# Output weights laid out four times by TensorE instead of by 16 transfers, the first token tiles' turned x read in place, and the last batch's tail cut in another order

## The chip, the core and the metric

One core of a Trainium2 chip runs the whole program. It has TensorE (PE; its weight loads are listed apart as PEld), VectorE (DVE), ScalarE (ACT), GpSimd (POOL), SyncE (SP, which here only issues transfers) and 16 DMA engines. The metric is the device time of one execution in microseconds, as the median of several.

## What is computed

The reference first pools x with 32 inducing vectors by softmax attention, lets x attend to the pooled vectors, and sends the outcome through a layer with a softmax-gated hidden vector and a layer norm:

```python
h   = mab(I, x)                 # per batch: 32 x 128, from 12608 x 128
a   = mab(x, h)                 # 12608 x 128: softmax(x h^T / sqrt(128)) h
hid = a @ w_in                  # 1024 wide
solu = hid * softmax(hid)
ln  = (solu - mean) / sqrt(var + 1e-6) * g_ln
out = ln @ w_out                # 128 wide
```

There are 4 batches of 12608 tokens, all in float32 but the weights, which come as float64 and are rounded to float32 in the kernel.

## The kernel before

A **tile** is 128 tokens; a batch has 98 tiles and one half tile, 99 in all. The program is not written in the order in which it runs. A planner (class Planner) holds, for each engine, the operations that could start, with a cost in ns and a priority (smaller goes first), and emits them one by one; each engine then runs its own list strictly in that order and waits where an operand is late. So a constant changed in a cost or a priority moves instructions on all engines.

**Stage p1** (function p1) reads x in groups (12 tiles in batch 0, 16 later), turns it by TensorE (L629 in batch 0, by PE row groups at L597 later), copies it out of PSUM (L575, L608), stores the turned x to DRAM (L642), and keeps a running maximum, sum and pooled vector (scores L668, maximum L694, small steps L699 to L738, exponentials L758, transposition L778, gather L784, accumulation L816). Batch 0 has its whole p1 ahead of everything else; batch b+1's p1 groups are started by tile number while batch b runs, the first at tile P1_FROM, then every P1_STEP tiles. **combine** ends a batch's p1: it makes h (copied at L853) and h @ w_in (L867, copied to hs at L870).

**Stage p2** takes tiles in groups (4, 12, then 16): it loads the turned x back from DRAM (L899), makes scores (L919), transposes them on DVE (L926), reduces, subtracts on POOL (L931), exponentiates on ACT (L938), turns the weights by PE (L961) and copies them to aT (L976).

**Per tile** (functions main and soft), in this order: PE makes the hidden vector aT x hs (L1115, called mm1 below); DVE scales it and takes its extreme (L1157); ACT exponentiates (L1168); POOL multiplies (L1172); ACT sums the squares (L1183); DVE transposes into a group buffer vt (L1196). Four tiles are a **group** (the last of a batch has three); when all four are in vt, PE multiplies them with the output weights (L1244, called products below): 32 steps of 32x129 matmuls, with two of the four PE row groups for either half w. There are three vt buffers. mm1 uses two row groups and can run beside a products half.

**Finishing** (functions evacuate, finish, stored): products are copied from PSUM to SBUF (L1272, by DVE or ACT), and for FG = 5 groups together the layer norm's factor is worked out in some ten small steps on ACT and POOL (L1297 to L1311). It needs the tile statistics, which go through DRAM to change their layout (dd at L1213, dl at L1221). Then each group is scaled (L1318 on POOL, or L1322 on ACT) and stored (L1334; the three-tile group by six small stores, L1348).

**Weights** (functions rounded, weights_in, weights_out): float64 bits are turned to float32 by DVE (L424 to L433, L442), ACT (L435) and POOL (L438, L440, L445). w_out uses the same scratch buffers after w_in. Then ACT multiplies by g_ln (L467), PE takes the column means (L476), DVE subtracts them (L481), and 16 transfers (L497) lay the 128x1024 array out four times into wc, so that each PE row group has its copy. An Event wc_ready holds back the first products until then:

```python
for a in range(4):
    for q in range(4):
        c = yield dma(M * FF * 4, lambda: nc.sync.dma_start(rows[a*M:(a+1)*M, :, q, :C], wg[q*M:(q+1)*M]), d, o, issue=600, prio=LATE)
```

PSUM is used as eight early banks until batch 0's p1 is done; handover then frees them and makes four wide ones (Lock H), in which all later scores, mm1 outputs and products lie.

## Time and profile before

| | us |
|---|---|
| median of three timed runs | 1212.05 (1209.96 to 1212.18) |
| the profiled execution, its own time | 1207.19 |
| its span, first to last instruction | 1205.3 |

The profile shows one execution. A line such as L1244 is a line of the kernel before. "Idle before" names what ended an engine's wait. PE counts two records for each float32 matmul instruction. A granted clock of 1.00 is 2.4 GHz, 0.50 is 1.2 GHz. A PE that is busy is not PE at its peak, since two row groups count as much as four.

### The profile page before, as it was taken

What the parts mean: (1) busy time and instruction counts of PE and PEld (TensorE: products, weight loads), DVE (VectorE), ACT (ScalarE), POOL (GpSimd) and SP (SyncE); (2) the same over time, 40 slices, a digit from 0 to 9 for tenths busy, and PEclk for the clock granted to TensorE, in tenths of its full rate; (3) what the DMA queues carried; (4) which work ended last, traced back from release to release, by engine and by line L of the source; (5) the groups of instructions that cost most, each with busy time, mean ns of one, the idle gap of its engine ahead of it and who ended that gap; (6) DMA issues with size and microseconds to landing.
All of it is one profiled execution on the core that took longest, in us unless ns stands there. A gap on an engine that the chain in (4) does not pass through costs nothing. (4 is left out here: it accounts for less than half of the span.)

```text
span 1205.3 us, 78134 instructions
## 1 busy us (share of the span) xinstructions
PE 1159.9 (96%) x35487; PEld 1079.9 (90%) x35487; DVE 1098.2 (91%) x1701; ACT 1119.5 (93%) x2263; POOL 1050.5 (87%) x599
## 2 busy tenths in 40 slices
PE   9899999999999999999999999999999999999995
PEld 7679899998998999999889989989899999999995
DVE  5789989999998999999999999999999899999992
ACT  5598989999999999999999999999999999999994
POOL 2578879798999789899898889989899999999995
PEclk9959999999999999999999999999999999999998
DMA  9770433232324343323225243334121321212023
GB/s 352 256 211 11 131 90 110 83 107 61 83 63 130 100 115 110 109 67 93 54 69 153 76 140 111 84 100 119 40 70 18 83 66 20 75 21 49 5 49 87
DMA packets 171725, 113.63 MB, mean 94 GB/s; under 512 B 79072, under 2 KB 136320, under 8 KB 171264
## 3 DMA queue, kind: packets, MB, share of 16 engines
q1 hardware_dynamic: 171392, 108.63, 31.2%
q8 instruction: 277, 4.54, 1.6%
q14 instruction: 56, 0.46, 0.1%
HBM read 54.30 MB, written 52.18 MB: 88 GB/s over the span
## 5 line engine op out<-in xcount | busy, mean ns | idle before, releaser
L1244 PE MATMUL h<-wc,vt 32*128 32x129 f32 (+1 forms) x25600 | 996.2, 274 | 15.5 <-issue 6.2
L1244 PEld LDWEIGHTS h<-wc,vt 32*128 32x128 f32 (+1 forms) x25600 | 961.3, 185 | 46.9 <-issue 27.3
L1172 POOL TENSOR_TENSOR eu<-hn,eu 128x1024 f32<-128x1024 f32 x197 | 464.1, 2374 | 34.6 <-ACT eu L1168 33.9
L1115 PE MATMUL h<-hs,aT 32*128 32x128 f32 x6336 | 438.4, 278 | 7.2 <-DVE spare L1157 1.7
L1115 PEld LDWEIGHTS h<-hs,aT 32*128 32x128 f32 x6336 | 393.2, 190 | 26.2 <-issue 6.7
L1196 DVE STREAM_TRANSPOSE vt<-eu 128x1024 f32<-128x1024 f32 x330 | 402.2, 1230 | 7.6 <-POOL eu L1172 7.5
L1183 ACT ACTIVATE sq<-eu 128x1024 bf16<-128x1024 f32 x330 | 346.1, 1049 | 6.2 <-POOL eu L1172 1.9
L1172 POOL TENSOR_TENSOR eu<-spare,eu 128x1024 f32<-128x1024 f32 x133 | 314.1, 2373 | 35.3 <-ACT eu L1168 35.3
L1157 DVE TENSOR_SCALAR_CACHE_REDUCE spare<-h,rn 128x1024 f32<-128x1024 f32 x198 | 248.3, 1261 | 26.3 <-PE h L1115 12.4
L1157 DVE TENSOR_SCALAR_CACHE_REDUCE hn<-h,rn 128x1024 f32<-128x1024 f32 x198 | 248.1, 1261 | 15.9 <-PE h L1115 7.9
L1168 ACT ACTIVATE eu<-hn,nm 128x1024 f32<-128x1024 f32 x197 | 224.4, 1139 | 1.6 <-DVE hn L1157 1.0
L1172 POOL TENSOR_TENSOR spare<-spare 128x1024 f32<-128x1024 f32 x65 | 154.5, 2376 | 20.3 <-ACT spare L1168 19.4
L1168 ACT ACTIVATE eu<-spare,nm 128x1024 f32<-128x1024 f32 x133 | 151.5, 1139 | 0.6 <-DVE spare L1157 0.3
L1196 DVE STREAM_TRANSPOSE vt<-spare 128x1024 f32<-128x1024 f32 x66 | 81.0, 1228 | 0.0
L1168 ACT ACTIVATE spare<-spare,nm 128x1024 f32<-128x1024 f32 x65 | 74.0, 1138 | 0.3 <-DVE spare L1157 0.3
L1183 ACT ACTIVATE sq<-spare 128x1024 bf16<-128x1024 f32 x66 | 69.2, 1049 | 1.2 <-ACT sq L1183 0.4
L1318 POOL TENSOR_TENSOR spare<-spare,fin 128x512 f32<-128x512 f32 x61 | 61.8, 1040 | 1.5
L1183 ACT ACTIVATION_READ_ACCUMULATOR sq<-eu 128x1 f32 x330 | 62.6, 190 | 0.0
L597 PE MATMUL h<-ident,xn 32*128 32x32 f32 x1188 | 54.4, 227 | 0.5 <-issue 0.5
L597 PEld LDWEIGHTS h<-ident,xn 32*128 32x128 f32 x1188 | 51.1, 141 | 0.7 <-issue 0.4
L1272 ACT COPY spare<-h 128x774 f32<-128x774 f32 (+3 forms) x57 | 36.6, 644 | 13.2 <-PE h L1244 9.5
L1322 ACT ACTIVATE spare<-spare,fin 128x128 f32<-128x128 f32 x156 | 47.9, 390 | 0.8 <-POOL fin L1311 0.7
(165 smaller groups left out, 832.4 us busy)
## 6 DMA issues: line engine op xcount, KB each, us to landing
xT<-xd SPq DMA_DIRECT2D x96, 256.0 KB, 4.1
out_dram<-spare SPq DMA_DIRECT2D x96, 256.0 KB, 3.7
xn<-in_x_dram SPq DMA_DIRECT2D x73, 256.0 KB, 4.0
xd<-xT SPq DMA_DIRECT2D x72, 256.0 KB, 2.8
dl<-dd SPq DMA_DIRECT2D x396, 1.0 KB, 2.8
xd<-vt SPq DMA_DIRECT2D x7, 768.0 KB, 10.4
spare<-in_x_dram SPq DMA_DIRECT2D x5, 768.0 KB, 14.4
wc<-hn SPq DMA_DIRECT2D x16, 128.0 KB, 3.3
```

What stands on the lines that cost most here:

```text
L597: nc.tensor.transpose(out=tr[:, k * 512 + s * M : k * 512 + (s + 1) * M], in_=xn[r, s, :], identity=ident[r, r])
L1115: nc.tensor.matmul(hp[:, cols], lhsT=aT[rows, i // 2, :], rhs=hs[rows, cols], start=True, stop=True)
L1157: lambda: nc.vector.tensor_scalar(out=hn, in0=hp, scalar1=rn, scalar2=None, op0=ALU.mult, op1=ALU.min, accum_out=nm),
L1168: "ACT", 1133, lambda: nc.scalar.activation(e, hn, AF.Exp, bias=nm, scale=-1.0, accum_out=G["qe"][:, s, 1:2]), d, rel, srel,
L1172: d = yield Op("POOL", 2330, lambda: nc.gpsimd.tensor_tensor(out=e, in0=hn, in1=e, op=ALU.mult), de, prio=t + PR_MU)
L1183: "ACT", 1040, lambda: nc.scalar.activation(sq, e, AF.Square, scale=1.0 / 32.0, accum_out=G["qe"][:, s, 0:1]), d,
L1196: lambda: nc.vector.transpose(out=G["vtb"][:, : n * FF].rearrange("p (j s t) -> p j s t", j=M, s=n)[:, :, s, :], in_=e.rearrange("p (a f) ...
L1244: nc.tensor.matmul(op[:rows, a - 2 * w, :], lhsT=vt[q, k, :], rhs=wc[q, k, :], start=(k == 0), stop=(k == JB - 1))
L1272: return lambda: eng(to, at)
L1318: return lambda: eng.tensor_tensor(out=raw, in0=raw, in1=y[:, i0 : i0 + 4].unsqueeze(2).to_broadcast([rows, 4, C]), op=ALU.mult)
L1322: act(raw[:, a, :], raw[:, a, :], AF.Copy, scale=y[:, i0 + a : i0 + a + 1])
```

## The change

Seven things change; lines named from here to the end of this section are those of the changed kernel.

1. w_out has scratch buffers of its own (conv2, made of buffers that p2 and mm1 use later), so its rounding no longer waits for w_in's; its load and g_ln's go out among the first x loads. In rounded, the last step is one DVE instruction (L454) in place of a DVE compare and two POOL multiplications.
2. The four copies of w_out are made by eight matmuls with a 0/1 matrix (L544) into early PSUM banks and eight copies from PSUM (L522), four on ACT and four on DVE as planned. The ones column of wc is set once the first two p1 groups are done, and handover waits for wc_ready.
3. p2 of batch 0 has groups of 4 and 8, and reads these 12 tiles' turned x from the SBUF buffer of the first p1 group. The first group's scores and its turn (whole array, L1026) use early banks. Stores of batch 0's turned x wait until all of batch 0's x is loaded.
4. In the last batch the three-tile group comes before the last full one, and the last finish has that one group alone, the one before it four.
5. Full-group stores of batches 0 to 2 take one of the four transfer tokens (BULK) that x loads, turned-x stores and turned-x loads share.
6. The planner's costs of p1 and p2 steps and its priorities are other numbers; mm1 may pick among the next three tiles (WINDOW_TILES), PE's idle time is filled with dummy transposes only where it is over 800 ns (FILL), and the scaling of finished groups has a priority of its own (OS_PRIO).
7. FOLD, EV_LATE, NR_POOL, OS_LATE are 0 and do nothing.

```diff
-OS_PRIO = None
+OS_PRIO = 0.0
...
-FILL = 400
+FILL = 800
-P1_FROM = 3
+P1_FROM = 6
-P1_STEP = 10.5
+P1_STEP = 13
-PR_EX = -2
+PR_EX = -8
 PR_EV = -20
-PR_FI = 40
-PR_G2 = 4
-PR_HN = -4
-PR_MU = 0
-PR_SQ = 1
-PR_TU = 4
+PR_FI = 10
+PR_G2 = 8
+PR_HN = 4
+PR_MU = -4
+PR_SQ = -4
+PR_TU = 12
 RUSH = -100.0
-SLACK = {"PE": 0, "ACT": 400, "DVE": 200, "POOL": 100, "SP": 0}
+SLACK = {"PE": 0, "ACT": 400, "DVE": 100, "POOL": 100, "SP": 0}
...
-WINDOW_TILES = 1
+WINDOW_TILES = 3
-OP_FIRST = -100
+OP_FIRST = -30
-WIN = -17.5
+WIN = -18.5
...
-    start = min(FIRST, some[0][1] - 1)
-    at_groups = [[(0, start), (start, some[0][1] - start)] + some[1:]] + [some] * (NB - 1)
+    start = min(FIRST, PG0 - 1)
+    first = [(0, start), (start, PG0 - start)]
+    at_groups = [first + [(PG0 + s, n) for s, n in cut(NT - PG0, AG, GS)]] + [some] * (NB - 1)
```

In rounded, and where w_out's buffers are lent:

```diff
...
-        k = yield Op("DVE", 602, lambda: ts(out=keep, in0=mag.bitcast(I32), scalar1=float(0x38100000), scalar2=None, op0=ALU.is_ge), g)
-        plan.set(free["mag"], k)
-        for c in cuts:
-            g = yield Op("POOL", 1180, lambda: gt(out=dst[:, c], in0=dst[:, c], in1=keep[:, c], op=ALU.mult), g, k)
+        g = yield Op(
+            "DVE", 1150,
+            lambda: stt(out=dst, in0=mag.bitcast(I32), scalar=float(0x38100000), in1=dst, op0=ALU.is_ge, op1=ALU.mult), g, m,
+        )
+        plan.set(free["mag"], g)
...
-    conv = [eu_b[:, :2, :].rearrange("p a f -> p (a f)"), eu_b[:, 2, :], eu_b[:, 3, :], eu_b[:, 4, :], hn_b[1]]
+    def flat(b):
+        return b.rearrange("p s t -> p (s t)")
+    conv = [flat(eu_b[:, :2, :]), eu_b[:, 2, :], eu_b[:, 3, :], eu_b[:, 4, :], hn_b[1]]
+    conv2 = [hs_all, a4_b.rearrange("p s r m -> p (s r m)"), flat(aT_b[0][0]), hn_b[0], flat(aT_b[1][0])]
...
+    def lend(lock, bufs, *events):
+        done = []
+        for e in events:
+            d = yield e
+            done += d
+        for b in bufs:
+            give(lock, b, *done)
...
+        gd = yield dma(4096, lambda: nc.sync.dma_start(g_sb, g_ln.rearrange("(k p) -> p k", p=P)), prio=WOUT_X)
+        for lock, bufs, at in ((HW, hw_b, ("raw",)), (A4, [a4_b], ("bits",)), (AT, aT_b, ("rest", "mag")), (HN, hn_b[:1], ("power",))):
+            spawn(lend(lock, bufs, *[conv2_free[k] for k in at]), WOUT)
+        g = yield from rounded(wg2, w_out.bitcast(U32).rearrange("(k p) d -> p k d", p=P), conv2, None, conv2_free, WOUT_X)
...
+        yield turned[NP[0] - 1]
+        mp, rel = yield EARLY_PB.at(LATE)
```

The layout of the output weights, and what stands in p1's store and in p2:

```diff
...
-        for a in range(4):
+        half = KC // 2
+        last, laid = [], [o]
+
+        def out_of(eng, sp, q, k0):
+            return lambda: eng(rows[:, k0 : k0 + half, q, :C], sp.rearrange("p (k d) -> p k d", k=half))
+
+        def laid_out(sp, q, k0, dp):
+            dc = yield Op(
+                "ACT", 570, out_of(nc.scalar.copy, sp, q, k0), dp, o, prio=LATE,
+                alt=Op("DVE", 620, out_of(nc.vector.tensor_copy, sp, q, k0), dp, o, prio=LATE),
+            )
+            give(EARLY_PB, sp, dc)
+            laid.append(dc)
+            if len(laid) == 9:
+                plan.set(wc_ready, *laid)
...
+        def spread(k0):
+            four, free = [], []
             for q in range(4):
-                c = yield dma(
-                    M * FF * 4,
-                    lambda: nc.sync.dma_start(rows[a * M : (a + 1) * M, :, q, :C], wg[q * M : (q + 1) * M]), d, o, issue=600, prio=LATE,
-                )
-                spread.append(c)
-        give(HN, wg2, *spread)
-        plan.set(wc_ready, *o_end, *spread)
+                sp, rel = yield EARLY_PB.at(LATE)
+                four.append(sp)
+                free += rel
+
+            def copies():
+                for q, sp in enumerate(four):
+                    r = slice(q * M, (q + 1) * M)
+                    nc.tensor.matmul(sp, lhsT=fold2[r, :], rhs=wg2[r, k0 * C : (k0 + half) * C], start=True, stop=True)
+
+            dp = yield Op("PE", 1200, copies, d, free, prio=LATE)
...
         def store():
+            here = []
+            for e in loaded if early else ():
+                d = yield e
+                here += d
...
-                d = yield dma((c1 - c0) * P * C * 4, go, ready, trel)
+                d = yield dma((c1 - c0) * P * C * 4, go, ready, trel, here)
...
-            d = yield Op("DVE", 225, spread, d)
+            d = yield Op("DVE", 475, spread, d)
...
+        early = b == 0 and j == 0
+        bank = EARLY_PB if early else H
+        if b == 0 and s0 + n <= PG0:
+            rel = yield early_xT["ready"]
+            xT = early_xT["tile"][:, s0 : s0 + n, :]
+            d = rel
...
-        d = yield Op("PE", SWITCH + n * 60, scores, d, rel, hd)
-        give(X2, xT, d)
-        d = yield Op("DVE", 66 + 33.4 * n, lambda: nc.vector.transpose(out=s2[:, :n, :].rearrange("p s m -> p (s m)"), in_=sp[:, : n * M]), d, srel)
+        d = yield Op("PE", (80 if early else SWITCH) + n * 60, scores, d, rel, hd)
+        if b == 0 and s0 + n <= PG0:
+            plan.set(early_xT[s0], d)
+        else:
+            give(X2, xT, d)
+        d = yield Op("DVE", 100 + 38 * n, lambda: nc.vector.transpose(out=s2[:, :n, :].rearrange("p s m -> p (s m)"), in_=sp[:, : n * M]), d, srel)
...
+        def turned_whole():
+            tr, trel = yield bank
+
+            def turn():
+                for q in range(pairs):
+                    both = a4[:, 2 * q : 2 * q + 2].rearrange("t s r m -> t (s r m)")
+                    nc.tensor.transpose(out=tr[:, q * P : (q + 1) * P], in_=both, identity=ident)
+
+            dt = yield Op("PE", 108.7 * pairs, turn, de, trel)
+            d = yield Op(
+                "ACT", 94 + 96 * pairs,
+                lambda: nc.scalar.copy(aT[:, :pairs, :], tr[:, : pairs * P].rearrange("p (q t) -> p q t", t=P)), dt, rel,
+            )
+            give(bank, tr, d)
```

The last batch's order, the scaling's priority and cost, the stores, handover:

```diff
...
+    order, fins = [], []
+    for b in range(NB):
+        js = list(range(NG))
+        if b == NB - 1 and NG > 1 and ff_groups[-1][1] < GS:
+            js[-2:] = js[:-3:-1]
+        order.append(js)
+        cuts = [js[i : i + FG] for i in range(0, NG, FG)]
+        if b == NB - 1 and len(cuts[-1]) > 1:
+            cuts[-1:] = [cuts[-1][:-1], cuts[-1][-1:]]
+        fins.append(cuts)
...
-            done = yield Op("POOL", 1000, scaled(nc.gpsimd), dy, prio=OS_PRIO, alt=Op("ACT", 1010, each_quarter, dy, prio=OS_PRIO) if OS_ACT else None)
+            done = yield Op("POOL", 1000, scaled(nc.gpsimd), dy, prio=OS_PRIO, alt=Op("ACT", 1170, each_quarter, dy, prio=OS_PRIO, late=OS_LATE) if OS_ACT else None)
...
-            d = yield dma(n * P * C * 4, lambda: nc.sync.dma_start(to, os), done)
+            mild = b < NB - 1
+            trel = (yield BULK)[1] if mild else ()
+            d = yield dma(n * P * C * 4, lambda: nc.sync.dma_start(to, os), done, trel, issue=1150)
+            if mild:
+                give(BULK, None, d)
...
+        for e in (early_turned, wc_ready):
+            d = yield e
+            done += d
```

**DVE where batch 0's h is made.** In the rows of the kernel before, L426 to L433 round w_out (eu is its scratch), L846 and L847 belong to combine, and the copy to h_0 releases the first p2 scores:

```order
L426 TENSOR_SCALAR eu<-eu 128x1024
L846 TENSOR_SCALAR small_121<-bank_e_74 128x1
L847 RECIPROCAL small_121<-small_121 128x1
L428 TENSOR_SCALAR hn_81<-eu 128x1024
L816 SCALAR_TENSOR_TENSOR acc_126<-acc_126,small_120,bank_e_76 128x128
L429 SCALAR_TENSOR_TENSOR eu<-eu 128x1024
L853 COPY h_0_116<-bank_e_74 128x128
L430 SCALAR_TENSOR_TENSOR eu<-eu 128x1024
L433 TENSOR_SCALAR eu<-eu 128x1024
```

In the changed kernel, at the same place (L506 subtracts the column means, L522 copies the laid-out weights from PSUM, L833 to L882 end p1, L912 and L913 belong to combine):

```order
L506 TENSOR_TENSOR hn_82<-bank_e_75,hn_82 128x1024
L882 SCALAR_TENSOR_TENSOR acc_125<-acc_125,small_122,bank_e_79 128x128
L833 TENSOR_SCALAR l_124<-l_124,small_119 128x1
L843 MEMSET eT 64x32
L844 STREAM_TRANSPOSE ew<-eT 128x224
L522 COPY wc<-bank_e_76 128x4x128
L522 COPY wc<-bank_e_75 128x4x128
L882 SCALAR_TENSOR_TENSOR acc_125<-acc_125,small_119,bank_e_74 128x128
L912 TENSOR_SCALAR small_120<-bank_e_76 128x1
L913 RECIPROCAL small_120<-small_120 128x1
L522 COPY wc<-bank_e_79 128x4x128
L919 COPY h_0_117<-bank_e_76 128x128
```

All of w_out's rounding stands farther ahead in the changed list; the subtraction and three of DVE's four weight copies now stand ahead of the copy to h_0, which is L919, and the fourth follows it.

**DVE at the first change of batch**, changed kernel, a little after the copy to h_1 (L1271 is the scaling, L1310 the transposition, L1001 and L1003 p2's first steps, L1095 and L1099 its last):

```order
L1001 STREAM_TRANSPOSE s_0_87<-h_716 128x512
L1003 TENSOR_REDUCE mx_88<-s_0_87 128x16
L1310 STREAM_TRANSPOSE vt<-eu 128x32x32
L1271 TENSOR_SCALAR hn_81,nm_112<-h_716,rn_97 128x1024
L1310 STREAM_TRANSPOSE vt<-eu 128x32x32
L1271 TENSOR_SCALAR hn_80,nm_113<-h_713,rn_97 128x1024
L1095 TENSOR_REDUCE nr_89<-a_93 128x16
L1271 TENSOR_SCALAR hn_82,nm_114<-h_716,rn_97 128x1024
L1099 RECIPROCAL rn_95<-nr_89 128x16
L1310 STREAM_TRANSPOSE vt<-eu 128x32x32
L1310 STREAM_TRANSPOSE vt<-spare 128x32x32
L1001 STREAM_TRANSPOSE s_1_90<-h_713 128x512
```

Between p2's first step and the first scaling of batch 1 (with rn_95, three rows farther on) stand three scalings; in the kernel before 19 scalings stand there.

**SP at the very end.** The kernel before (dl_110 belongs to the last finish, which has five groups):

```order
L1213 DMA dd_105<-qe_104 128x8
L1221 DMA dl_110<-dd_105 32x4x2 x4
L1213 DMA dd_107<-qe_106 128x6
L1334 DMA out_dram<-spare 512x1x128
L1221 DMA dl_110<-dd_107 32x4x2 x3
L1334 DMA out_dram<-spare 512x1x128 x8
L1348 DMA out_dram<-spare 96x128
L1348 DMA out_dram<-spare 32x128
L1348 DMA out_dram<-spare 64x128 x2
L1348 DMA out_dram<-spare 32x128 x2
```

The changed kernel (dl_110 belongs to the finish of four groups, dl_108 to the last one):

```order
L1327 DMA dd_103<-qe_102 128x8
L1336 DMA dl_110<-dd_103 32x4x2 x4
L1327 DMA dd_105<-qe_104 128x6
L1336 DMA dl_110<-dd_105 32x4x2 x3
L1327 DMA dd_107<-qe_106 128x8
L1336 DMA dl_108<-dd_107 32x4x2 x4
L1451 DMA out_dram<-spare 512x1x128 x3
L1467 DMA out_dram<-spare 96x128
L1467 DMA out_dram<-spare 32x128
L1467 DMA out_dram<-spare 64x128 x2
```

Before, nine stores of two finishes and six small ones stand at the end; now the last finish has one store, behind three full and six small ones of the finish before it (the last of the small ones and that one store follow the rows shown). At DVE's end, the copy of the three-tile group's products now stands ahead of the last transposition, and both halves of the last group's products are copied by DVE; before, DVE's list ended with one half of either of the last two groups.

## Rows read from the trace of the kernel before

**Rows 1.** The page's first lines: span, and busy time of each engine with its share of the span.

```profile
span 1205.3 us, 78134 instructions
PE 1159.9 (96%) x35487; PEld 1079.9 (90%) x35487; DVE 1098.2 (91%) x1701; ACT 1119.5 (93%) x2263; POOL 1050.5 (87%) x599
```

**Rows 2.** Busy time by stretch: after the stretch and its length come PE, PEld, DVE, ACT and POOL busy us (and instructions), the granted PE clock, the DMA engines' share, GB/s.

```profile
10.00:20.00 10.00, 10.00 (x126) 7.25 (x125) 7.72 (x27) 6.25 (x16) 0.52 (x2) 1.00 1.04 393
20.00:30.00 10.00, 10.00 (x145) 6.81 (x143) 7.57 (x25) 8.20 (x20) 5.71 (x6) 1.00 1.03 409
30.00:40.00 10.00, 8.99 (x136) 6.80 (x135) 8.14 (x38) 5.02 (x17) 2.86 (x3) 1.00 1.04 403
50.00:60.00 10.00, 8.60 (x128) 7.47 (x126) 9.17 (x16) 7.72 (x18) 8.58 (x7) 0.80 0.54 180
60.00:70.00 10.00, 10.00 (x126) 6.45 (x122) 7.28 (x11) 8.60 (x14) 6.37 (x4) 0.52 0.71 191
70.00:80.00 10.00, 9.27 (x144) 9.03 (x144) 9.84 (x23) 8.79 (x19) 7.08 (x4) 0.66 0.96 254
80.00:90.00 10.00, 8.66 (x114) 6.73 (x114) 8.11 (x12) 9.91 (x18) 10.00 (x6) 0.50 0.64 192
200.00:300.00 100.00, 99.50 (x3065) 91.66 (x3061) 96.33 (x160) 96.34 (x193) 85.18 (x44) 1.00 0.29 79
```

**Rows 3.** Timeline of PE between the first mm1 and the first products: start, length, line, out<-in, records, idle before.

```profile
49.74 2.28 PE L1115 MATMUL h<-hs,aT 32*128 32x128 f32 x48 [0.55 <-ACT aT L976]
...
55.30 3.08 PE L476 MATMUL h<-hn,ones_mean 128*128 128x128 f32 x16 [1.40 <-ACT hn L467]
...
69.82 1.72 PE L1115 MATMUL h<-hs,aT 32*128 32x128 f32 x32
...
75.81 4.48 PE L1115 MATMUL h<-hs,aT 32*128 32x128 f32 x48
81.63 1.94 PE L919 MATMUL h<-xT,h 128*32 128x512 f32 x8 [1.34 <-DMA xT<-xd]
83.50 4.42 PE L1244 MATMUL h<-wc,vt 32*128 32x129 f32 x56
```

**Rows 4.** Timeline of DVE in the same stage.

```profile
40.85 1.22 DVE L429 SCALAR_TENSOR_TENSOR eu<-eu 128x1024 uint32<-128x1024 uint32 x1
41.99 0.28 DVE L853 COPY h<-bank_e 128x128 f32<-128x128 f32 x1
...
49.50 0.66 DVE L442 TENSOR_SCALAR eu<-hn 128x1024 f32<-128x1024 int32 x1
...
58.45 1.21 DVE L481 TENSOR_TENSOR hn<-h,hn 128x1024 f32<-128x1024 f32 x1
...
78.08 1.24 DVE L1196 STREAM_TRANSPOSE vt<-eu 128x1024 f32<-128x1024 f32 x1
```

**Rows 5.** Timelines of ACT (first two), POOL and SP in that stage.

```profile
30.57 0.59 ACT L575 COPY vt<-bank_e 128x512 f32<-128x512 f32 x1 [1.01 <-PE bank_e L629]
...
53.43 2.43 ACT L467 ACTIVATE hn<-hn,g_sb 128x128 f32<-128x128 f32 x8
50.30 2.50 POOL L445 TENSOR_TENSOR hn<-hn,eu 128x512 f32<-128x512 f32 x2 [0.72 <-DVE eu L442]
59.80 2.73 SPq L497 DMA_DIRECT2D wc<-hn  x4
...
70.30 4.04 SPq L497 DMA_DIRECT2D wc<-hn  x6
```

**Rows 6.** What PE's weight loads waited for between 92 and 1167 us: total us, times, longest.

```profile
PEld h L1244 <- ACT spare L1272: 7.2, 11, 1.4
PEld h L1115 <- DVE hn L1157: 5.1, 12, 0.8
PEld h L1115 <- DVE spare L1157: 4.5, 11, 0.8
```

**Rows 7.** Timeline of DVE: small steps of a 16-tile p1 group and the transposition of a 16-tile p2 group.

```profile
64.17 0.72 DVE L926 STREAM_TRANSPOSE s<-h 128x512 f32<-128x512 f32 x1 [1.06 <-PE h L919]
...
71.28 0.46 DVE L710 TENSOR_REDUCE small<-small 32x1 f32<-32x1 f32 x3
```

**Rows 8.** One p2 group in mid run: the DVE transposition, and the last copy of the turned weights on ACT.

```profile
340.74 0.67 DVE L926 STREAM_TRANSPOSE s<-h 128x512 f32<-128x512 f32 x1
...
347.06 0.58 ACT L976 COPY aT<-h 128x512 f32<-128x512 f32 x1
```

**Rows 9.** The end: the chain's last run of products, then the timelines of DVE, ACT, POOL and SP.

```profile
1169.96 14.59 PE h L1244 x512
1191.98 0.42 DVE L1272 COPY spare<-h 96x258 f32<-96x258 f32 x1 [6.92 <-PE h L1244]
1192.56 0.31 ACT L1297 ACTIVATE fin<-dl,tiny 128x20 f32<-128x20 f32 x1 [0.15 <-DMA dl<-dd]
1195.62 3.04 POOL L1318 TENSOR_TENSOR spare<-spare,fin 128x512 f32<-128x512 f32 x3
1189.93 9.38 SPq L1334 DMA_DIRECT2D out_dram<-spare  x8
1199.41 3.87 SPq L1348 DMA_DIRECT2D out_dram<-spare  x6
```

**Rows 10.** The page's part 6: full-group stores, number, KB each, median us from issue to landing.

```profile
out_dram<-spare SPq DMA_DIRECT2D x96, 256.0 KB, 3.7
```

More of the change, by code (lines that the diff above doesn't have):

```diff
@@ new lines, in laid_out @@
+        def laid_out(sp, q, k0, dp):
[9 more added lines that the diff above has]
+            four, free = [], []
+            for q in range(4):
+                sp, rel = yield EARLY_PB.at(LATE)
[6 more added lines that the diff above has]
+            dp = yield Op("PE", 1200, copies, d, free, prio=LATE)
+            last.append(dp)
+            if len(last) == 2:
+                give(HN, wg2, *last)
+            for q, sp in enumerate(four):
+                spawn(laid_out(sp, q, k0, dp), LATE)
@@ L503, in fill @@
+        for k0 in (0, half):
+            spawn(spread(k0), LATE)
     def fill(bank):
@@ L540, in set_attention_then_solu_kernel @@
     gathers, pooled_in = {}, {}
+    loaded = [Event() for _ in range(NP[0])]
+    early_turned = Event()
+    early_xT = {"tile": None, "ready": Event(), **{s0: Event() for s0, n in at_groups[0] if s0 + n <= PG0}}
     def p1(b, k):
@@ L561, in p1 @@
                 xd.append((d, c0))
+        if early:
+            plan.set(loaded[k], *[d for d, at in xd])
         if k == 0:
@@ L634, in p1 @@
             plan.set(turned[k])
-        yield copied
+        got = yield copied
+        if early and not k:
+            early_xT["tile"] = xT
+            plan.set(early_xT["ready"], *got)
         def store():
+            here = []
+            for e in loaded if early else ():
+                d = yield e
+                here += d
             wrote = []
@@ L722, in p1 @@
         prev = yield chain[b][k]
-        if early:
+        if folded:
             d = yield Op(
-                "DVE", 122,
+                "DVE", 245,
                 lambda: nc.vector.tensor_scalar(
@@ L760, in exps @@
                 )
-        de = d = yield Op("ACT", (100 + 30 * n) * len(parts) + (0 if first else 190), exps, dm, erel)
+        de = d = yield Op("ACT", (200 + 30 * n) * len(parts) + (0 if first else 235), exps, dm, erel)
         def total(eng):
@@ L943, in p2 @@
         ways, copied, read = [0, 1], [], []
+        def turned_whole():
[8 more added lines that the diff above has]
+                lambda: nc.scalar.copy(aT[:, :pairs, :], tr[:, : pairs * P].rearrange("p (q t) -> p q t", t=P)), dt, rel,
+            )
+            give(bank, tr, d)
+            plan.set(early_turned, d)
+            yield turned_too
+            give(A4, a4, dt, *turned_too.after)
+            for s in range(n):
+                plan.set(aT_ready[(b, s0 + s)], *turned_too.after, d)
+            plan.set(A["all"], d)
         def turned_rows():
@@ L992, in p2, with norms @@
         turned_too = Event()
-        for _ in range(2):
+        if early:
+            assert n % 2 == 0 and pairs <= 4
+            spawn(turned_whole(), PRIO_P2(b, j))
+        for _ in range(0 if early else 2):
             spawn(turned_rows(), PRIO_P2(b, j))
-        d = yield Op("DVE", 66 + 33.4 * n, lambda: nc.vector.tensor_reduce(out=nr[:, :n], in_=a4[:, :n, 0, :], op=ALU.add, axis=AX.X), de)
+        def norms(eng):
+            return lambda: eng.tensor_reduce(out=nr[:, :n], in_=a4[:, :n, 0, :], op=ALU.add, axis=AX.X)
+        d = yield Op("POOL", 60 + 61.4 * n, norms(nc.gpsimd), de) if NR_POOL else Op("DVE", 66 + 33.4 * n, norms(nc.vector), de)
         d = yield Op("ACT", 100, lambda: nc.scalar.activation(nr[:, :n], nr[:, :n], AF.Copy, scale=-1.0, bias=-1e-9), d)
@@ L1082, in main @@
         for b in range(NB):
-            for j in range(NG):
+            for j in order[b]:
                 left = list(range(ff_groups[j][1]))
@@ L1124, in main @@
                     left.remove(s)
-                    if not left and j == NG - 1:
+                    if not left and j == order[b][-1]:
                         give(HW, hT[b], d)
@@ L1274, in evacuate @@
         d = yield Op(
-            "DVE", 71 + 269 * n, copied(nc.vector.tensor_copy), dop, rel, prio=prio,
+            "DVE", 71 + 269 * n, copied(nc.vector.tensor_copy), dop, rel, prio=prio, late=EV_LATE,
             alt=Op("ACT", 72 + 193 * n, copied(nc.scalar.copy), dop, rel, prio=prio),
@@ L1281, in evacuate @@
         if not F["left"]:
-            spawn(finish(b, js[0] // FG), prio + PR_FI)
+            spawn(finish(b, f), prio + PR_FI)
     def finish(b, f):
         F = fin[(b, f)]
-        js = [j for j in range(NG) if j // FG == f]
+        js = fins[b][f]
         rows = ff_groups[js[0]][1] * M
@@ L1382, in handover @@
             d = yield xd_done[(0, k)]
+            done += d
+        for s0, n in first:
+            d = yield early_xT[s0]
             done += d
```

146 lines of the change are left out of this document (77 added, 69 removed).

## Prediction

> **What bounds the kernel now.** I read the page's totals first, to see which engine could bound: PE is busy 96% of a span of 1205.3 us, ACT 93%, DVE 91%, POOL 87% [rows 1]. Such shares are means, so I went on to the stretches. In mid run, 200 to 300 us, PE is busy 99.50 of 100 us at full clock, ACT and DVE 96.3 each [rows 2]. There the kernel is bound by PE with two engines close behind, and an edit that only moves work can win little. Between 50 and 90 us it is otherwise: PE is still busy 8.6 to 10 of each 10 us, but the granted clock is 0.80, 0.52, 0.66 and 0.50, near 1.2 GHz instead of 2.4 [rows 2]. That stage runs from the first mm1 at 49.74 to the first products at 83.50 [rows 3].
>
> In the timelines of that stage I looked for what each engine waits for. PE waits 1.40 us for ACT's gains ahead of the column means (which take 3.08 us at the low clock), and 1.34 us for a transfer of turned x ahead of the last scores before the products [rows 3]. On DVE, h is copied at 41.99, and half of w_out's rounding follows it: a pass at 49.50, the subtraction at 58.45; the fourth transposition, which completes the first group, ends at 79.32 [rows 4]. ACT's gains take 2.43 us, POOL's multiplications of a weight 2.50 us, and SP issues the 16 transfers from 59.80 to 74.34 [rows 5]. These transfers are all issued 9 us before the products start, and the products follow straight on a scores matmul [rows 3]: nothing on the path waits for them, so their removal is worth nothing by itself.
>
> From 92 us on, PE's weight loads wait little: 7.2 us for PSUM copies on ACT, 5.1 and 4.5 us for the scalings on DVE [rows 6]. Those three, 16.8 us in 1075, are about all that a better order of DVE and ACT could win there.
>
> **The change, part by part: the early stage.** Rounding w_out earlier puts its DVE work ahead of h. Before, three passes of 0.66 and one of 1.22 stood ahead: 3.2 us. Now all four short passes (2.6), three long ones (the new combined step, which the trace lacks, counted as L429: 3.7), the subtraction (1.2) and three of the four weight copies stand there. The last are 128x512 copies out of PSUM: ACT's row for one is 0.59 us [rows 5], and DVE's transposition of that size 0.72 [rows 7]; I take 0.6 each, 1.8 together. That is 9.3 us, and w_in's own combined step adds 0.6 (1.22 for 0.66): 6.7 us more ahead of h. DVE is idle 2.3, 2.4 and 1.9 us in the three stretches from 10 to 40 us [rows 2], 6.6 in all, so h could be late by nothing; but that idle time comes in pieces between dependent steps, and in the new list DVE must wait for gains, means and eight matmuls before h's turn comes. I take h 6 us later, at 48, and the first mm1 at 55; bounds are +0 and +10.
>
> Behind the first mm1, PE loses work. Of the 33.8 us up to the products go the means (3.08), both waits (1.40 and 1.34) and one tile's mm1 of the three in 4.48 us (1.5), since the first products stand one tile earlier in the list. One more scores matmul comes in (1.94). That leaves 28.4 us, so the products start at 55 + 28.4 = 83.4: **where they started before, term 0**. Bounds: −5, if the clock does not fall, and then DVE decides: from the copy's end to the fourth transposition's end is 37.0 us now, of which 6.7 go ahead of h, so 48 + 30.3 = 78.3. And +5, if h is 4 to 5 us later still.
>
> Against this stands a rule. The Trainium skill, "TensorEngine Tiling (Array Packing)", section Performance Considerations (PSUM Bottleneck), says that packing matmuls into parts of the array speeds up TensorE but not the emptying of PSUM, which can then be the bottleneck. By our row the eight copies are 2.4 us on either of two engines, 4.7 on one; by the rule they, not the matmuls, decide how long the new layout takes. No run here has shown it yet.
>
> **The planner's numbers.** The old costs were too low for what DVE does: three small copies of a p1 step were planned at 225 ns and take 0.46 us, a 16-tile transposition planned at 600 takes 0.72 [rows 7]. The new ones (475 and 708) are near the trace, so the orders of DVE and ACT should fit better. The most to win is in the 16.8 us of [rows 6]; **I take −2**, an eighth, with 0 and −8 (half) as bounds. Against it, counted over the whole lists, the changed program has 14 product or mm1 steps of PE more, because fewer find a partner. A step is 14.59/64 = 0.23 us [rows 9], so +3.2 at most; ACT takes six PSUM copies over from DVE, ACT being as full as DVE. I set these at 0 within the −2, bound +3.2.
>
> **Change of batch.** In the new list only three scalings and five transpositions stand between p2's first step and the next batch's first scaling, where 19 scalings stood. One long DVE pass is 1.22 to 1.24 us [rows 4], so eight and the small steps between give about 12.4 us of cover. The chain that it must hide, from the transposition's start at 340.74 to the last copy of turned weights, ends at 347.64 [rows 8]: 6.9 us, and one mm1 of 1.5 makes 8.4. Cover remains, some 4 us, for queueing; **term 0**, bound +5 in all.
>
> **The end.** After the last copy starts (1191.98) the span runs 13.3 us: copy, 3 us of small steps, POOL's scaling of three groups in 3.04 us, and a queue of stores on SP: eight at 1.17 us each, then six small ones for 3.87 us [rows 9]. In the changed list one group is left: two copies on DVE (0.84), the small steps (1192.56 to 1195.62, 3.06), one scaling (1.0), one store issued and landed in 3.7 us [rows 10]: 8.6, or 4.7 less. But the three-tile group's copy now stands ahead of DVE's last transposition, and waits for its products; I charge 1.2 for it and the waits between. **Term −3.5**, bounds −5 and −1. The store's queue is the risk: three full and six small stores ahead of it, 3 x 1.17 + 3.87 = 7.4 us, are ready some 4 us after the three-tile group's copy, and finish about 12 us after it; the last group needs 7.3 us of products (half of 14.59), 0.84, 3.06 and 1.0, also 12.2. It just fits.
>
> **Stores under a token and later stores of turned x.** In mid run the DMA engines are 0.29 busy [rows 2]; a store of 3.7 us that waits for a token waits for nothing that PE needs: 0.
>
> **Sum:** 0 − 2 + 0 − 3.5 = −5.5 on the profiled execution, 1207.2 to 1201.7. The median stood 4.9 us above that execution, so 1206.6; I say 1206.5.
>
> **The rivals.** (a) *The clock stays up in the early stage.* The means at the low clock and two PE waits are gone, which speaks for it; against it, mm1 by row groups still runs there, and the clock fell with PE busy 10 of 10 us. Products at 78.3, 5 us more: 1201.5. (b) *The layout of w_out holds back h.* DVE waits in its list for a chain over ACT, PE, DVE and PE, and PSUM copies come ahead of h. If h comes at 52, the early stage takes back 4 us: 1210.5, within 0.2%. The skill's rule above points to this one. (c) *Slower: a stall at every change of batch.* If p2's chain, which runs between p1's last steps and other tiles, takes longer than its cover of 12.4 us, PE has no tile to go on with, three times. It decides from (1214.5 − 1206.5)/3 = 2.7 us each; at 4 us each, 1218.5. For it: the cover was cut from 19 scalings. Against it: 4 us of spare by the measured chain. (d) *The tail is not shorter.* If the six small stores hold SP beyond the last scaling by 3 us, the term is −0.5: 1209.5.
>
> **How the numbers follow.** Two measurements of this kernel within 0.2%, 2.4 us, cannot be told apart. Chances: the forecast 0.50, (a) 0.10, (b) 0.18, (c) 0.15, (d) 0.07. Faster is nine tenths of the forecast, (a), and half of (d): 0.58. Slower is (c), a quarter of (b) whose delay grows beyond 8 us, and a part of the forecast's own spread: 0.23. The rest, 0.19, is no change. The forecast's own range is 1201 to 1211. With (a) and its planner's gain at the bound of −4 or so below, and (b) and (c) above, the range is 1197 to 1217.
>
> **What the new profile would show.** If right: h copied near 48, first products near 83, a granted clock again near 0.5 before them; the end 9 to 10 us behind the last copy's start; PE's waits for scalings and copies under 15 us; no PE gap over 2 us where batches change. Wrong would be a products' start off by over 4 us, a PE wait for DVE or ACT behind each batch's first scores, or a longer 200 to 300 us stage in which ACT ends what PE waits for.

## The result and the profile after

The changed kernel is slower: 1215.4 us (1210.38 to 1226.61) beside 1209.8 us for the kernel before (1205.35 to 1212.41), twenty runs each; ratio 1.0053, 95% interval 1.0037 to 1.0069. Its profiled execution took 1215.05 us, 7.9 more than that of before. The forecast was 1206.5.

The page's first lines, and the same stretches as in [rows 2] (columns as there, PE's granted clock behind POOL):

```profile
span 1213.3 us, 78043 instructions
PE 1163.2 (96%) x35498; PEld 1083.6 (89%) x35498; DVE 1099.4 (91%) x1701; ACT 1124.4 (93%) x2283; POOL 1047.2 (86%) x596
...
50.00:60.00 10.00, 8.47 (x130) 5.46 (x130) 7.81 (x18) 6.89 (x16) 4.54 (x4) 1.00 0.29 82
60.00:70.00 10.00, 9.19 (x150) 7.46 (x150) 10.00 (x17) 9.67 (x18) 10.00 (x6) 0.91 0.71 233
70.00:80.00 10.00, 10.00 (x100) 6.22 (x98) 7.22 (x11) 9.39 (x15) 9.51 (x6) 0.50 0.33 111
200.00:300.00 100.00, 97.92 (x3212) 93.28 (x3208) 93.15 (x150) 96.50 (x199) 92.02 (x52) 1.00 0.33 91
700.00:800.00 100.00, 94.66 (x2934) 88.77 (x2930) 90.22 (x144) 94.10 (x194) 86.21 (x50) 0.95 0.34 102
```

Before, 700 to 800 us read PE 98.30, DVE 95.13, ACT 97.25, POOL 91.23 and a clock of 1.00. Now each of the four is 3 to 5 us less busy there, and the granted clock is 0.95.

**The early stage** did what was forecast, by a somewhat other path. PE from the first mm1 to the first products, then DVE and ACT around the laying out of w_out and the copy of h (start, length, line, out<-in, idle before):

```profile
52.62 2.28 PE L1229 MATMUL h<-hs,aT 32*128 32x128 f32 x48
...
79.73 7.35 PE L1359 MATMUL h<-wc,vt 32*128 32x129 f32 x206
45.41 1.29 DVE L522 COPY wc<-bank_e 128x512 f32<-128x512 f32 x2 [0.52 <-PE bank_e L544]
47.63 0.69 DVE L522 COPY wc<-bank_e 128x512 f32<-128x512 f32 x1 [0.41 <-PE bank_e L544]
48.34 0.29 DVE L919 COPY h<-bank_e 128x128 f32<-128x128 f32 x1
66.40 1.20 DVE L1310 STREAM_TRANSPOSE vt<-eu 128x1024 f32<-128x1024 f32 x1
45.46 1.08 ACT L522 COPY wc<-bank_e 128x512 f32<-128x512 f32 x2 [2.75 <-PE bank_e L544]
```

h is copied at 48.34 (forecast 48), the first mm1 at 52.62 (55), the first products at 79.73 (83.4, before 83.50). But the first transposition of a tile comes at 66.40, where before it came at 56.9. At 100 us POOL has 992.6 us of busy time still to come, where it had 994.6 before: two us ahead, not four.

**The end** is shorter than forecast. SP, and the last scaling on POOL:

```profile
1200.48 3.02 SPq L1336 DMA_DIRECT2D dl<-dd  x4
1203.60 1.92 SPq L1451 DMA_DIRECT2D out_dram<-spare  x3
1205.61 3.75 SPq L1467 DMA_DIRECT2D out_dram<-spare  x6
1209.64 0.57 SPq L1451 DMA_DIRECT2D out_dram<-spare  x1
1208.57 1.04 POOL L1433 TENSOR_TENSOR spare<-spare,fin 128x512 f32<-128x512 f32 x1
```

From the end of the last products (1205.1) to the span's end (1213.3) are 8.2 us; before it was 13.4 (1192.0 to 1205.3).

**What is lost lies between**: from 100 us to the last products 1092.0 us before, 1105.1 now, 13.1 more. These two stretches as a whole, before and now, then the third quarter of the products, before and now (L1244 and L1359 alone, so only PE and PEld):

```profile
100.00:1192.00 1092.00, 1068.75 (x34136) 1006.13 (x34128) 1023.91 (x1523) 1046.15 (x2103) 990.70 (x549) 1.00 0.29 79
100.00:1205.10 1105.10, 1071.09 (x34056) 1010.61 (x34051) 1018.64 (x1514) 1052.41 (x2128) 990.70 (x551) 0.99 0.29 80
659.20:941.20 282.00, 250.10 (x6401) 241.39 (x6400) 1.00 0.30 85
657.50:951.90 294.40, 257.20 (x6402) 247.30 (x6400) 0.98 0.31 89
```

Of the 13.1 us, 10.8 are idle time of PE and 2.3 busy time. They are not spread evenly. There are 25600 records of products, 6400 a batch. Half of them are done at 657.5 us now and at 659.2 before, with three tiles' mm1 fewer done at that time. The third quarter, batch 2, takes 12.4 us more, the last one 2.4 more. In second profiles of both kernels (e14 and e15 below) the third quarter takes 293.6 and 283.2 us.

PE's waits between 92 and 1167 us, in the changed kernel (total us, times, longest):

```profile
PE h L1359 <- issue: 11.2, 21, 1.4
PE h L1229 <- issue: 4.5, 9, 1.2
PE h L1359 <- ACT spare L1387: 6.9, 10, 1.1
PE h L1359 <- ACT xT L666: 2.5, 2, 1.7
```

and in the kernel before:

```profile
PE h L1244 <- issue: 6.2, 11, 1.2
PE h L1115 <- issue: 1.4, 3, 0.7
PE h L1244 <- ACT spare L1272: 4.8, 9, 1.2
```

In all, PE is idle 33.6 us there, 23.1 before, and 19 waits are of 0.7 us or more where there were 7. "Issue" is time for which the profile shows nothing that PE waited for: 15.7 us in the rows above, 7.6 before, so most of the rise has no named cause. Around some of the waits the granted clock is at half for a while. Stretches of 10 us of the changed kernel around four such waits (the same columns):

```profile
750.00:760.00 10.00, 8.79 (x238) 8.41 (x234) 8.48 (x17) 7.31 (x16) 8.07 (x4) 0.83 0.06 5
776.00:786.00 10.00, 8.07 (x171) 7.50 (x168) 8.17 (x10) 8.74 (x20) 6.91 (x6) 0.66 0.33 109
1055.00:1065.00 10.00, 8.84 (x224) 8.65 (x224) 9.40 (x13) 9.94 (x23) 9.53 (x7) 0.83 0.06 4
1127.00:1137.00 10.00, 8.89 (x222) 8.51 (x222) 10.00 (x14) 10.00 (x21) 10.00 (x5) 0.83 0.17 37
```

0.83 over 10 us is half clock in 3.4 of them. Summed over 100 to 1180 us, the clock is at 1.2 GHz for 20.5 us in this profile, and for 3.4 before.

### The profile page after: what moved, and what is told of

Read it like the earlier page. It is cut to its first block, busy times and chain, and to the rows that moved or that the text cites. A ratio compares the mean times of both kernels' runs of the same rounds, so it can differ in the third digit from the quotient of the medians.

```text
span 1213.3 us, 78043 instructions
## 1 busy us (share of the span) xinstructions
PE 1163.2 (96%) x35498; PEld 1083.6 (89%) x35498; DVE 1099.4 (91%) x1701; ACT 1124.4 (93%) x2283; POOL 1047.2 (86%) x596
## 5 line engine op out<-in xcount | busy, mean ns | idle before, releaser
L1359 PE MATMUL h<-wc,vt 32*128 32x129 f32 (+1 forms) x25600 | 1002.6, 274 | 25.9 <-issue 11.6
L1359 PEld LDWEIGHTS h<-wc,vt 32*128 32x128 f32 (+1 forms) x25600 | 968.9, 186 | 56.9 <-issue 33.3
L1310 DVE STREAM_TRANSPOSE vt<-eu 128x1024 f32<-128x1024 f32 x330 | 402.5, 1231 | 10.5 <-POOL eu L1286 9.3
L1271 DVE TENSOR_SCALAR_CACHE_REDUCE spare<-h,rn 128x1024 f32<-128x1024 f32 x198 | 248.8, 1264 | 26.1 <-PE h L1229 13.2
L1271 DVE TENSOR_SCALAR_CACHE_REDUCE hn<-h,rn 128x1024 f32<-128x1024 f32 x198 | 248.9, 1261 | 23.8 <-PE h L1229 12.9
L1286 POOL TENSOR_TENSOR spare<-spare 128x1024 f32<-128x1024 f32 x66 | 157.0, 2378 | 14.5 <-ACT spare L1282 14.4
L1310 DVE STREAM_TRANSPOSE vt<-spare 128x1024 f32<-128x1024 f32 x66 | 80.8, 1225 | 0.7 <-POOL spare L1286 0.6
L1387 ACT COPY spare<-h 128x774 f32<-128x774 f32 (+3 forms) x63 | 40.5, 646 | 16.1 <-PE h L1359 10.9
## 6 DMA issues: line engine op xcount, KB each, us to landing
xd<-vt SPq DMA_DIRECT2D x7, 768.0 KB, 10.2
```

Source lines behind the costliest of these rows:

```text
L1271: lambda: nc.vector.tensor_scalar(out=hn, in0=hp, scalar1=rn, scalar2=None, op0=ALU.mult, op1=ALU.min, accum_out=nm),
L1286: d = yield Op("POOL", 2330, lambda: nc.gpsimd.tensor_tensor(out=e, in0=hn, in1=e, op=ALU.mult), de, prio=t + PR_MU)
L1310: lambda: nc.vector.transpose(out=G["vtb"][:, : n * FF].rearrange("p (j s t) -> p j s t", j=M, s=n)[:, :, s, :], in_=e.rearrange("p (a f) ...
L1359: nc.tensor.matmul(op[:rows, a - 2 * w, :], lhsT=vt[q, k, :], rhs=wc[q, k, :], start=(k == 0), stop=(k == JB - 1))
L1387: return lambda: eng(to, at)
```

## The experiments

What is compared below: the ratio to the kernel before, and of the profile the time from 100 us to the last products (**stretch**; 1092.0 before), the time in it at half clock up to 1180 us (3.4 before), and the time from the last products to the end (**tail**; 13.4 before). The number of PE steps of products and mm1 in the list, and of those without a partner on the other row groups, is counted in the program (4443 and 402 before, 4457 and 432 changed). Stretch, half clock and tail are those of one execution each: e4_tailonly and e12_tail5 have the list of before up to the last batch, and their stretches read 1096.3 and 1093.3.

| run | ratio, 95% interval | stretch | half clock | tail | steps, alone |
|---|---|---|---|---|---|
| changed | 1.0053 (1.0037 to 1.0069) | 1105.1 | 20.5 | 8.2 | 4457, 432 |
| e1_allback | 1.0101 (1.0078 to 1.0123) | 1103.1 | 13.7 | 15.3 | 4469, 456 |
| e2_costback | 1.0050 (1.0033 to 1.0067) | 1105.5 | 20.5 | 8.3 | 4473, 464 |
| e3_prioback | 1.0182 (1.0163 to 1.0200) | 1116.4 | 33.3 | 15.4 | 4462, 442 |
| e4_tailonly | 1.0015 (0.9997 to 1.0034) | 1096.3 | 3.4 | 15.3 | 4443, 402 |
| e5_nobulk | 1.0049 (1.0025 to 1.0073) | 1103.9 | 18.4 | 8.4 | 4494, 506 |
| e6_groups | 1.0068 (1.0048 to 1.0088) | 1096.1 | 3.4 | 13.7 | 4482, 480 |
| e7_beforebulk | 1.0070 (1.0045 to 1.0096) | 1096.3 | 10.2 | 13.1 | 4470, 456 |
| e8_neighbour | 1.0045 (1.0024 to 1.0067) | 1096.9 | 3.4 | 14.0 | 4469, 454 |
| e9_tail_lastfi | 0.9993 (0.9972 to 1.0015) | 1098.1 | 10.2 | 7.9 | 4455, 426 |
| e10_refit | 1.0058 (1.0038 to 1.0077) | 1101.6 | 13.7 | 8.4 | 4424, 366 |
| e11_tailfit | 1.0015 (0.9994 to 1.0036) | 1093.4 | 3.4 | 8.8 | 4434, 384 |
| e12_tail5 | 0.9977 (0.9957 to 0.9998) | 1093.3 | 6.8 | 7.8 | 4443, 402 |
| e13_stalls | 1.0121 (1.0090 to 1.0151) | 1108.4 | 13.7 | 13.1 | 4443, 402 |
| e14_after_again | one profile | 1104.3 | 20.5 | 8.2 | 4457, 432 |
| e15_before_again | one profile | 1090.9 | 3.4 | 13.2 | 4443, 402 |

**Are the planner's numbers at fault, or the structure?** Three versions of the changed kernel. In e1_allback all numbers are those of before, in e2_costback the costs alone, in e3_prioback the constants alone:

```diff
-P1_STEP = 13
+P1_STEP = 10.5
...
-            d = yield Op("DVE", 475, near, d, added)
+            d = yield Op("DVE", 225, near, d, added)
```

> The changed kernel with all of the planner's numbers of before (priorities, P1_FROM, P1_STEP, WINDOW_TILES, FILL, SLACK, OP_FIRST, OS_PRIO and the costs of p1 and p2 steps); the early stage, the last batch's order and the token for stores stay changed. Theory N (the planner's numbers cost the 17 us that the changed kernel loses between its first and its last products): the stretch from first to last products is again 1108 us as before, products start near 80, the end is 8 us behind them, and the time is about 9 us under before (some 1200 to 1202). Rival S (the structure costs it: the token for stores, and batch 0's p2 groups cut at other tiles): that stretch stays near 1125 us and the time near 1215. Rival L (any new order is as likely to be poor; the order of before was a lucky one): in between, 1205 to 1213.

> The changed kernel with only the planner's costs of p1 and p2 steps as before; its priorities stay changed. Theory N in its form costs: near 1202. If the priorities cost the time: near 1215, no change. Rival L: anything from 1205 to 1220 without a pattern.

> The changed kernel with only the priorities and the other constants as before (P1_FROM, P1_STEP, PR_, WINDOW_TILES, FILL, SLACK, OP_FIRST, OS_PRIO); the costs stay changed. Theory N in its form priorities: near 1202, stretch from first to last products near 1108. If the costs do it: near 1215. Rival L: 1205 to 1220 without a pattern.

Theory N falls: with the old numbers the changed structure is slower still (1.0101, with the constants alone 1.0182), and the costs alone make no difference (1.0050). The new constants are not what costs the time. What they win in this structure is the tail: it is 15.3 to 15.4 us with the old constants, 8.2 to 8.4 with the new, 7.1 less, and by the ratios the changed kernel is 5.8 us under e1_allback. Ahead of the tail they win nothing: the last products end at 1203.1 us with all numbers old, at 1205.1 with all new.

**The tail alone, on the kernel before** (order and fins as in the change, nothing else):

> The kernel before with only the last batch's order and the last two finishes as changed. If the tail is worth what the two traces show (13.4 us from last products to end before, 8.2 after): 5 us under before, 0.996; the stretch from first to last products stays 1108 us within 2. If the order of the last batch itself costs PE time ahead of the last products: between 0 and 5 us under.

No gain, and a tail of 15.3 us. SP shows why, then ACT's first step of the last finish (same columns):

```profile
1192.26 7.50 SPq L1347 DMA_DIRECT2D out_dram<-spare  x8
1199.86 0.58 SPq L1361 DMA_DIRECT2D out_dram<-spare  x1
1200.49 2.18 SPq L1234 DMA_DIRECT2D dl<-dd  x4
1204.05 0.30 ACT L1310 ACTIVATE fin<-dl,tiny 128x4 f32<-128x4 f32 x1 [4.71 <-DMA dl<-dd]
```

Eight stores stand on SP ahead of the last finish's loads of its statistics, so that finish begins at 1204.05, 8 us behind its products. In the changed kernel the five-group finish is done earlier (PR_FI 10 for 40), its stores are gone, and the loads come first.

**The token, the p2 groups, and a neighbour.** e5_nobulk is the changed kernel with `mild = False`; the other three are the kernel before with one thing changed:

```diff
+            trel = (yield BULK)[1] if mild else ()
...
+    at_groups = [first + [(PG0 + s, n) for s, n in cut(NT - PG0, AG, GS)]] + [some] * (NB - 1)
...
-P1_STEP = 10.5
+P1_STEP = 10.25
```

> The changed kernel, its full-group stores free of the transfer tokens again. Theory B (the loss between first and last products, 1125 us where before had 1108, comes from the token: stores take places of x loads and turned-x loads, and the planner starts p1 and p2 steps later for it): the stretch falls to about 1110 and the time to about 1200. Theory L (the order of before is a well-fitted one and any other list of the same work loses 10 to 20 us): no pattern, 1208 to 1222.

> The kernel before, with only batch 0's p2 groups cut as in the changed one (4, 8, then 16). Theory G (the other cut is what costs: p2's loads and steps fall at other tiles than p1's): slower by 10 us or more, stretch of products near 1120. Theory B: no change, 1207 to 1210. Theory L: slower by 5 to 15 us.

> The kernel before, with only the token for full-group stores (and its issue cost of 1150) as in the changed one. Theory B: slower by 10 us or more. Theory G: no change. Theory L: slower by 5 to 15 us.

> The kernel before with P1_STEP 10.25 for 10.5: the same work, p1 groups of batches 1 to 3 one or two tiles earlier from the third on. It gauges theory L. If L holds: 5 to 15 us slower than before. If the numbers of before are not a lucky point: within 3 us.

The token costs the changed kernel nothing that shows (1.0049 without it, 1.0053 with it). Theory G asked for a stretch near 1120 in e6_groups; it is 1096.1. But each of the three lists next to that of before is 0.45 to 0.70% slower, even where a number of the planner moved by 2% and the work is the same. So the list of before was better fitted than these three neighbours, and theory L holds for it: these three have 26 to 39 steps more, 5.9 to 8.9 us at 0.23, and measure 5 to 8.5 us.

**Fitted anew.** e9_tail_lastfi is e4_tailonly with priority 10 for the last batch's finishing steps; e11_tailfit is that with eight numbers fitted to its list; e10_refit is e2_costback with five:

> The kernel before with the last batch's order and finishes as changed, and, in the last batch alone, the finishing steps at the priority of the changed kernel (10 in place of 40). In the run with the last batch's order alone, eight stores stood ahead of the last finish's loads on SP, and the last products were followed by 15.5 us. Theory Q (SP's queue of the finish before is what holds the end, and the earlier finish clears it): 8 to 9 us from last products to end, time 2 to 4 us under before (the list has 4455 product and mm1 steps, 12 more than before, 2.7 us of the 5). If it is the order of the last batch's products itself: still over 12 us, and no faster than before.

> The changed kernel with the p1 and p2 costs of before and five numbers fitted anew to its list: P1_STEP 12, PR_FI 12, PR_TU 11, PR_EV -18, H_LAST -31. Its list has 4424 product and mm1 steps, 366 of them without a partner (the changed kernel 4457 and 432, before 4443 and 402). Theory F (the lists differ by how many steps of PE have a partner, and the numbers decide that, not the structure): 33 steps x 0.23 = 7.5 us less than the changed kernel, so 1 to 3 us under before. Rival W (the changed structure makes PE wait for ACT and DVE and its clock fall, whatever the list): still 4 to 7 us over before.

> The kernel of the run with the last batch's order and its finishing priority, with eight numbers fitted anew (PR_G2 3, PR_HN -2, PR_MU 5, PR_SQ 2, PR_TU 5, PR_EV -19, H_LAST -28, WINDOW_TILES 2): 4434 steps, 384 without a partner. Theory F: 21 steps x 0.23 = 4.8 us under that run, so 6 to 8 us under before, 0.994. Rival W or L (what a list is worth on the chip isn't told by its steps): within 3 us of before.

Theory Q holds for the tail, which falls to 7.9 us. The time does not follow: 2 to 4 us under before were expected, and it is 0.9993, not clear of 1, with a stretch 6.1 us longer. Theory F falls twice: with 33 steps fewer the changed structure is no faster (1.0058), and 21 fewer bring e11_tailfit nothing beside e9_tail_lastfi. Steps tell some of the lists next to that of before, not all lists.

**Waits and the clock.** By then the profiles showed one common thing: the stretch goes with the time at half clock in it. Over all runs of the table but e13_stalls the correlation is 0.96, and 0.71 us of stretch go with each us at half clock. This does not say which of the two makes the other. The six versions of the changed structure have 13.7 to 33.3 us of it, those of the structure before 3.4 to 10.2, e13_stalls again left out. e13_stalls puts 15 waits into the kernel before; e14 and e15 are the two kernels again; e12_tail5 confines priority 10 to the last five finishes:

```diff
+                        if now in STALLS:
+                            nc.tensor.matmul(hp[:, 0:1], lhsT=ident, rhs=ident[:, 0:1], start=True, stop=True)
+                            nc.vector.tensor_copy(held_up, hp[:, 0:1])
+                            nc.tensor.matmul(hp[:, 0:1], lhsT=ident, rhs=held_up, start=True, stop=True)
...
-            spawn(finish(b, f), prio + PR_FI)
+            spawn(finish(b, f), prio + (PR_FI if b < NB - 1 or f < len(fins[b]) - 5 else 10))
```

> The kernel before with the last batch's order and finishes as changed, and priority 10 for the last five finishes alone. Its list has the 4443 steps of before, 402 without a partner, and is that of before up to the last batch. Theory Q (the end is SP's queue; the rest of the list is what it was): 8 to 9 us from last products to end in place of 13.4, time 4 to 5 us under before, 0.996. If the order of the last products loses it again: within 2 us of before.

> The kernel before, with PE made to wait for DVE ahead of 15 of the 396 mm1 (tiles 60, 80, ... 340): one matmul column, a DVE copy of it, a matmul that reads it. The planner doesn't know, so the lists are those of before. Each wait should be 0.7 to 1.5 us. Theory C (waits of this size make PE's granted clock fall to half for a few us, and that is where the changed kernel loses its time): 4 or more falls to 0.50 between 100 and 1180 us, each behind such a wait, and 15 to 30 us over before, more than the waits' own sum. Rival N (a wait costs only itself, the falls in the changed kernel have another cause): no more falls than before (one), and a time of no more than the waits' sum, 10 to 20 us, less what the engines behind PE had in hand.

> The changed kernel itself, for another profile. If its list makes the long waits: again 4 to 6 falls of the clock between 100 and 1180 us, at the same places (437, 754, 778, 1058, 1130), and again 15 to 20 waits of PE of 0.7 us and more. If they come by chance from execution to execution: other places, another number.

> The kernel before itself, for another profile. If its list is what keeps waits rare: again one or two falls and about 7 waits of 0.7 us and more between 92 and 1167 us, last products 1092 us behind 100. If that profile was a lucky execution: 3 to 6 falls, last products 1096 to 1104.

The waits belong to the list. Rows of PE in the changed kernel's first profile:

```profile
753.29 0.38 PE L1359 MATMUL h<-wc,vt 32*128 32x129 f32 x2 [0.83 <-ACT spare L1387]
780.22 0.58 PE L1359 MATMUL h<-wc,vt 32*128 32x129 f32 x2 [1.71 <-ACT xT L666]
1057.57 0.73 PE L1359 MATMUL h<-wc,vt 32*128 32x129 f32 x8 [1.16 <-ACT aT L1072]
1128.86 1.23 PE L1229 MATMUL h<-hs,aT 32*128 32x128 f32 x16 [1.11 <-DVE hn L1271]
```

and in its second, e14_after_again:

```profile
750.45 0.38 PE L1359 MATMUL h<-wc,vt 32*128 32x129 f32 x2 [0.83 <-ACT spare L1387]
777.29 0.38 PE L1359 MATMUL h<-wc,vt 32*128 32x129 f32 x2 [1.76 <-ACT xT L666]
1054.78 1.02 PE L1359 MATMUL h<-wc,vt 32*128 32x129 f32 x6 [1.16 <-ACT aT L1072]
1127.42 0.82 PE L1229 MATMUL h<-hs,aT 32*128 32x128 f32 x10 [1.12 <-DVE hn L1271]
```

The same four waits, of the same size and for the same engines, and the clock falls about all four again; there are 18 long waits. The fifth place does not come again: at 437 us the first profile has a fall behind a wait of 1.05 us, the second has the wait, of 1.04, and no fall, but one at 225. The kernel before has one fall again, at another place (1078 us, first 1131), and 9 long waits.

The stalls settle less than was asked. Their waits were 0.25 to 0.82 us, shorter than meant. The time rose by 14.6 us (1.0121), about 1 us for each of 15, no more than the probes keep PE from its other work (0.9 to 1.5 us each, 15.7 in all; 226.38 to 227.40 us is the first). The profile has 10.2 us more at half clock than before, and the time shows no price for them; at 0.71 it would be 7 us. There were four falls in place of one; two stand right behind a probe:

```profile
813.95 0.38 PE L1122 MATMUL h<-held,ident 128*128 128x1 f32 x2 [0.55 <-DVE held L1121]
810.00:820.00 10.00, 8.96 (x194) 6.89 (x190) 7.65 (x12) 9.86 (x20) 8.08 (x6) 0.83 0.35 108
985.00:995.00 10.00, 8.92 (x209) 8.44 (x210) 7.47 (x13) 8.72 (x19) 8.87 (x6) 0.83 0.05 5
```

But these two have a second wait beside the probe's, of 0.50 and 0.66 us for ACT, and the other two falls stand behind pairs of ordinary waits (0.65 and 0.94, 0.80 and 0.55). So it is not shown that a probe's wait brings a fall by itself, and theory C's price is not shown either: what is shown is that these waits cost about their own length, and that this run, with more waits, had more falls.

e12_tail5 is the only run that is under the kernel before by more than its interval, and just so: 0.9977, interval 0.9957 to 0.9998, 1205.25 us beside 1208.77 on the same chip. Of the 5.6 us that its tail saves it keeps about 3, where 4 to 5 were expected.

## Why the prediction was wrong

**The step that failed is the term for the planner's numbers**, −2 with bounds 0 and −8, and +3.2 at most against it. But for the change of batch it stood for everything between the early stage and the end, and measured +13.1. Its bound was taken from the three waits of [rows 6], 16.8 us, as if a new order could only remove waits. These three did shrink, to 13.7 us in the changed kernel:

```profile
PEld h L1359 <- ACT spare L1387: 10.3, 16, 1.3
PEld h L1229 <- DVE hn L1271: 2.1, 3, 1.3
PEld h L1229 <- DVE spare L1271: 1.3, 3, 0.6
```

But the list is new for all 1075 us, and a new list adds waits in other places: PE is idle 10.8 us more in all, and three small changes to the kernel before (e6 to e8) cost 5 to 8.5 us each. That costs nearer to the trace make better orders was argued, not read from a row; e2_costback shows that the costs make no difference. Nor are the other numbers at fault, as e1_allback shows: the loss comes with the list that the changed structure has, whatever the numbers, and for that the sum had no term but the +3.2. The 17 us more at half clock, worth 8.5 at most, and the steps without a partner, 3.2 at most, would lengthen PE's busy time; that rose by 2.3 in all, and no run shows what either cost.

**The early stage, term 0**, held: h at 48.34, as worked out. Products started 3.7 us sooner than forecast, partly as rival (a) had it: the means ran at full clock, in 2.03 us instead of 3.08, and the clock fell only from 68 us on. Two us of it are left at 100 us, since the first tile's transposition came 9.5 us later than before. Rival (b) did not come. DVE waited for the matmuls (0.52 and 0.41 us), not for its copies out of PSUM, of 0.69 us each on DVE and 0.59 on ACT. By the Trainium skill's "TensorEngine Tiling (Array Packing)", Performance Considerations (PSUM Bottleneck), those copies could have become the bottleneck; this trace doesn't agree, for eight copies in four us.

**The end, term −3.5**: right in its mechanism, measured −5.2, just beyond its bound of −5. The store queue of rival (d) did not hold it (the six small stores are issued by 1209.36 us, the last scaling ends at 1209.61), but only because of PR_FI 10, which the prediction had not connected with the end: in e4_tailonly, with PR_FI 40, SP's queue took the whole term.

**Change of batch, term 0**, held: none of the long waits of the two profiles stands at a change of batch as a gap of over 2 us, so rival (c), the slower one, did not happen where it was put. **The token, 0**, held (e5_nobulk).

**The offset**: 4.9 us between profile and median was a matter of three runs; over twenty it is 2.6.

What stays open is why all six versions of the changed structure lose time ahead of the last products and have more time at half clock there. Long waits alone don't set them apart: e10_refit has 8 of 0.7 us or more, the runs of the structure before 6 to 10. It is not the token, the costs, the constants or the count of steps, and neither the groups, the token nor the tail alone does it to the kernel before. What is left is the early stage, by which all engines enter mid run in another phase, or several of the parts together; neither was tried. That the two kernels are level at half of their products, and part in batch 2, speaks against a loss right behind the early stage.

## To carry to other kernels

Where three engines are over 95% busy in mid run and an order of thousands of instructions has been fitted by its numbers, price any change that writes the whole list anew as a loss before its gains (0.45 to 0.70% in the three neighbours here), and measure neighbours of the old list to see how well it was fitted. Put a gain where it leaves the rest of the list alone: the tail by itself, with its priority set for the last finishes only, is what was worth keeping. And follow the last loads and stores on their queue: a finish that is late on another engine puts its stores ahead of what the end waits for.

## What was not expected of the hardware

In mid run, with PE 96% busy or more in every 100 us but two, the granted clock still fell to half, five times in the changed kernel and once in the one before, each time in a stretch with PE waits of 0.8 to 1.8 us; a 10 us stretch then reads 0.83 or 0.66. A wait of that size does not always do it: in the kernel before, 1.17 us at 605 us in one profile and 1.18 at 601 in the other passed at full clock. The mean clock of a whole run hides it (0.984 and 0.982 in the two profiles, the slower kernel having the higher one), because the kernel before spends more time at half clock in its first 100 us, 30.7 us beside 13.7.
